# Moving small elementwise work from VectorE to GpSimd, with a new instruction order, in a four-layer attention kernel

## The chip, the cores and the metric

The kernel runs on one core of one Trainium2 chip. The time is that of one execution in device microseconds (us); times below are medians of four executions unless it is said otherwise; the four of the kernel before lie within 0.5% of each other. VectorE (DVE), ScalarE (ACT), GpSimd (POOL) and TensorE (PE, its weight loads PEld) each have a list of instructions of their own, whose order the program fixes. "Granted clock" is the share of full TensorE speed that the records show.

## The reference

The input x has 2048 rows of 512 values and 32 heads of 16. Four layers, A B A B, each add attention(layernorm(x)) to x.

```python
# layer A: linear attention; pk is made from k in the same way
pq = einsum("bhsd,hdf->bhsf", q, w_phi)
phi_q = concat([softmax(pq), softmax(-pq)])
kv = einsum("bhsf,bhsd->bhfd", phi_k, v);  z = sum over s of phi_k      # over all rows
o = einsum("bhqf,bhfd->bhqd", phi_q, kv) / (einsum("bhqf,bhf->bhq", phi_q, z) + 1e-6)
# layer B: a window of 8 earlier rows at distance 0, 2, ... 14
attn = softmax(q . k[rows] * scale);  o = attn . v[rows]
# both
x = x + o @ wo
```

Only kv and z of layer A join all rows. Between these "global sums" a block of 512 rows can run ahead of the others.

## The kernel before

Rows are handled in four blocks b of 512. A step of a stage is a small closure. All steps are emitted in one fixed global order (the string `_ORDER`), which thereby fixes the list of every engine. `_CHOICE` says for each flexible step (emptying a PSUM bank, adding a residual, normalising) whether VectorE or ScalarE does it, and `_SLOTS` gives the buffers.

```python
for w in _ORDER.split():
    key = self.names[int(w, 36)]
    ...
    self.threads[key][i]()

# layernorm of the new x: mean and variance from two accumulated sums
def sq(t):     # ScalarE: sum of squares of a row, by accum_out
    nc.scalar.activation(out=sqd[:], in_=xb[:, t, :], func=ACT.Square, accum_out=T["ss"][:, t:t + 1])
def var(lo, n):
    u = T["sums"][:, lo:lo + n]
    nc.vector.scalar_tensor_tensor(out=q, in0=u, scalar=-1.0 / D, in1=u, op0=ALU.mult, op1=ALU.mult)
    nc.vector.tensor_tensor(out=q, in0=q, in1=ss, op=ALU.add)          # q, ss: slices, shortened here
def ln():      # ScalarE: lnv = Ln(scale * var + eps); rstd = Exp(-lnv / 2)
    ...
def nmr():     # VectorE: the shift, -mean * rstd
    nc.vector.scalar_tensor_tensor(out=U["nmr"][:, 0:n], in0=T["sum"](), scalar=-factor,
                                   in1=U["rstd"][:, 0:n], op0=ALU.mult, op1=ALU.mult)
# keys: sums of 16 exponentials in four levels t8, t4, t2, t1; the last one:
def t1(t, m):
    nc.vector.tensor_tensor(out=T["s1"][:, 0:m * G], in0=T["s2"][:, 0:m * G, 0], in1=T["s2"][:, 0:m * G, 1], op=ALU.add)
# query normaliser: dr multiplies the denominators (PSUM) by rS, then
    nc.vector.tensor_tensor(out=T["Ds"][:], in0=T["DR"][:, 0, :], in1=T["DR"][:, 1, :], op=ALU.add)
def rho():
    nc.vector.tensor_tensor(out=T["rho"][:], in0=self.rS[L, b][:],
                            in1=T["Ds"][:].unsqueeze(1).to_broadcast([P, 2, P]), op=ALU.mult)
```

The large VectorE work of layer B is `prod` (query times shifted keys) and `pav` (weights times shifted values): 128x4096 products, both inputs in SBUF, 2.3 us each and 2.2 us from start to start.

## Time and profile before

| | before |
|---|---|
| median of three executions | 330.5 us (329.39 to 330.88) |
| span of the profiled execution | 327.5 us |
| busy: PE, VectorE, ScalarE, GpSimd | 310.3, 302.2, 279.3, 25.3 us |
| VectorE idle (span less busy) | 25.3 us |

The page and its rows are shown in the prediction.

### The profile page before, as it was taken

The page shows a single profiled execution, that of the slowest core. Times are in us where ns is not written, and L with a number is a line of the kernel's source. Part 1 is how long each engine was busy: PE and PEld are TensorE (multiplying, and loading weights), DVE is VectorE, ACT ScalarE, POOL GpSimd, SP SyncE. Part 2 cuts the span into 40 slices and gives each one's busy share as a digit, 9 for nine tenths or more (in the row PEclk, how much of TensorE's full clock was granted, in tenths as well). Part 3 has the DMA queues.
Part 4 walks back from the last instruction along what each step waited for, and adds up shares of the span by engine and source line. Part 5 has one row for each costly group of instructions (what it writes and reads, how often), then busy time and mean ns, then how long its engine had stood idle before and what let it go on. Part 6 is the DMA issues. An engine that isn't in the chain of part 4 may idle for free. (4 is left out here: it accounts for less than half of the span.)

```text
span 327.5 us, 8033 instructions
## 1 busy us (share of the span) xinstructions
PE 310.3 (95%) x3176; PEld 149.5 (46%) x3203; DVE 302.2 (92%) x439; ACT 279.3 (85%) x634; POOL 25.3 (8%) x50
## 2 busy tenths in 40 slices
PE   7999999999999999999999999979999999999873
PEld 3655456445444444443444455644544454433221
DVE  7998995998998999899999999699999999999993
ACT  5999988998888999989999999798999996676550
POOL 4000000000021003000000000000000208400000
PEclk9999999999999999999999999999999999999999
DMA  7980000004556899998750300023436977679952
GB/s 197 380 197 3 0 2 4 2 20 120 105 148 135 152 164 133 139 121 154 137 135 1 67 3 2 4 59 90 128 58 125 179 146 134 150 139 158 166 176 92
DMA packets 37388, 35.41 MB, mean 108 GB/s; under 512 B 23008, under 2 KB 32224, under 8 KB 37344
## 3 DMA queue, kind: packets, MB, share of 16 engines
q1 hardware_dynamic: 36816, 34.81, 53.6%
q8 instruction: 27, 0.44, 0.6%
q14 instruction: 17, 0.14, 0.2%
q10 hardware_dynamic: 528, 0.02, 0.1%
HBM read 10.50 MB, written 2.36 MB: 39 GB/s over the span
## 5 line engine op out<-in xcount | busy, mean ns | idle before, releaser
L927 PE MATMUL ps<-xnT,WB 128*128 128x512 bf16 x384 | 87.6, 380 | 0.5 <-DMA xnT<-xn 0.5
L1081 DVE TENSOR_TENSOR pav<-PT,Vg 128x4096 bf16<-128x4096 bf16 (+1 forms) x34 | 72.0, 2162 | 1.5 <-DMA Vg<-V 1.0
L1019 DVE TENSOR_TENSOR prod<-QT,K 128x4096 bf16<-128x4096 bf16 x32 | 72.5, 2291 | 0.3 <-ACT QT L192 0.2
L927 PEld LDWEIGHTS <-WB 128*128 128x128 bf16 x384 | 42.3, 114 | 43.3 <-issue 5.8
L520 PEld LDWEIGHTS <-oT 128*128 128x128 bf16 x256 | 23.8, 97 | 34.5 <-ACT oT L192 5.7
L192 ACT CAST oT<-ps 128x512 bf16<-128x512 f32 (+1 forms) x60 | 32.1, 587 | 8.4 <-PE ps L1090 7.1
L706 ACT ACTIVATE Eq<-ps 128x512 bf16<-128x512 f32 x64 | 34.0, 615 | 0.7 <-PE ps L698 0.6
L520 PE MATMUL ps<-WoB,oT 128*128 128x512 bf16 x122 | 32.1, 380 | 2.4 <-ACT oT L192 2.0
L599 ACT ACTIVATE Ek<-ps 128x512 bf16<-128x512 f32 x64 | 33.6, 622 | 0.4 <-PE ps L593 0.2
L698 PE MATMUL ps<-xnT,WA 128*128 128x512 bf16 x128 | 30.7, 380 | 0.6 <-DVE Eq L816 0.6
L540 ACT ACTIVATE sqd<-x 128x512 bf16<-128x512 bf16 x48 | 30.1, 643 | 1.0 <-DVE x L533 0.8
L605 PE MATMUL ps<-WA,xnT 128*128 128x512 bf16 x120 | 30.0, 380 | 0.5 <-issue 0.2
L593 PE MATMUL ps<-WA,xnT 128*128 128x512 bf16 x124 | 29.7, 380 | 0.6 <-DMA xnT<-xn 0.2
L520 PE MATMUL ps<-WoA,oT 128*128 128x512 bf16 x120 | 29.2, 380 | 0.4
L533 DVE SCALAR_TENSOR_TENSOR x<-ps,x 128x512 bf16<-128x512 f32 x38 | 25.4, 686 | 1.9 <-PE ps L520 1.7
L192 ACT CAST V<-ps 128x512 bf16<-128x512 f32 x31 | 17.5, 595 | 4.4 <-PE ps L927 4.3
L192 ACT CAST K<-ps 128x512 bf16<-128x512 f32 x31 | 17.8, 585 | 3.7 <-PE ps L927 3.3
L530 ACT ACTIVATE x<-ps 128x512 bf16<-128x512 f32 x26 | 15.1, 598 | 6.4 <-PE ps L523 6.3
L192 ACT CAST QT<-ps 128x512 bf16<-128x512 f32 x29 | 17.1, 592 | 2.5 <-PE ps L927 2.5
L651 DVE TENSOR_TENSOR Ek<-Ek,rk 128x4096 bf16<-128x4096 bf16 (+1 forms) x10 | 18.6, 1858 | 0.5 <-ACT rk L646 0.5
L593 PEld LDWEIGHTS <-xnT 128*128 128x128 bf16 x128 | 12.1, 97 | 15.4 <-DMA xnT<-xn 0.7
L446 ACT ACTIVATE xn<-x,nmr,rstd 128x512 bf16<-128x512 bf16 x23 | 18.2, 822 | 1.0 <-DVE nmr L435 0.8
(129 smaller groups left out, 433.3 us busy)
## 6 DMA issues: line engine op xcount, KB each, us to landing
Vg<-V SPq DMA_DIRECT2D x128, 131.5 KB, 4.4
Prho<-rd SPq DMA_DIRECT2D x8, 512.0 KB
x<-in_A_x_dram SPq DMA_DIRECT2D x3, 512.0 KB
WB<-in_B_wqkv_dram SPq DMA_DIRECT2D x3, 512.0 KB, 11.6
wraw<-in_A_wqkv_dram SPq DMA_DIRECT2D x4, 256.0 KB, 4.5
out_dram<-x SPq DMA_DIRECT2D x4, 256.0 KB, 2.2
out_dram<-x SPq DMA_DIRECT2D x8, 128.0 KB, 2.2
x<-in_A_x_dram SPq DMA_DIRECT2D x4, 128.0 KB
```

Source lines behind the costliest of these rows:

```text
L192: self.nc.scalar.copy(out=out, in_=in_)
L520: nc.tensor.matmul(y[:], lhsT=oT[:, c, t * P:(t + 1) * P], rhs=Wo()[:, c, :], start=(c == 0), stop=(c == NB - 1 and not onpe))
L533: nc.vector.scalar_tensor_tensor(out=xb[:, t, :], in0=T[t][:], scalar=1.0, in1=xb[:, t, :], op0=ALU.mult, op1=ALU.add, **kw)
L540: nc.scalar.activation(out=sqd[:], in_=xb[:, t, :], func=ACT.Square, accum_out=T["ss"][:, t:t + 1])
L593: nc.tensor.matmul(pk[:], lhsT=xnT[:, t, k, :], rhs=self.WA[:, k, D:2 * D], start=(k == 0), stop=(k == NB - 1))
L599: nc.scalar.activation(out=T["E"][:, t, s, :], in_=T["k", t][:], func=ACT.Exp, scale=1.0 - 2.0 * s)
L605: nc.tensor.matmul(pv[:], lhsT=xnT[:, t, k, :], rhs=self.WA[:, k, 2 * D:3 * D], start=(k == 0), stop=(k == NB - 1))
L698: nc.tensor.matmul(pq[:], lhsT=self.WA[:, k, hb * P:(hb + 1) * P], rhs=xnT[:, :, k, :], start=(k == 0), stop=(k == NB - 1))
L706: nc.scalar.activation(out=self.Eq[L, b][s][:, :, hb, :], in_=T[hb][:].rearrange("p (t i) -> p t i", t=4), func=ACT.Exp, scale=1.0 - 2.0 * s)
L927: nc.tensor.matmul(pp[:], lhsT=self.WB[:, k, i * D + c:(i + 1) * D:NB], rhs=xnT[:, :, k, :], start=(k == 0), stop=(k == NB - 1))
L1019: nc.vector.tensor_tensor(out=pr[:], in0=QT[:, c:c + 1, :].to_broadcast([P, NW, TB]), in1=win, op=ALU.mult)
L1081: nc.vector.tensor_tensor(out=pv, in0=PT[:, :, lo:lo + n].unsqueeze(1).to_broadcast([P, NB, 2, n]), in1=vw, op=ALU.mult)
```

## The change

The intent: VectorE is near full and GpSimd nearly empty, so small elementwise work goes to GpSimd wherever no global sum waits for it. The core of the diff, with cuts:

```diff
         def var(lo, n):
-            nc.vector.scalar_tensor_tensor(out=T["q"]..., in0=u, scalar=-1.0 / D, in1=u, op0=ALU.mult, op1=ALU.mult)
-            nc.vector.tensor_tensor(out=T["q"]..., in0=T["q"]..., in1=T["ss"]..., op=ALU.add)
+                nc.gpsimd.tensor_tensor(out=w, in0=u, in1=u, op=ALU.mult)
+                nc.gpsimd.tensor_scalar(out=q, in0=ss, scalar1=float(D), scalar2=None, op0=ALU.mult)
+                nc.gpsimd.tensor_tensor(out=q, in0=q, in1=w, op=ALU.subtract)     # 12 places; scale 1/(D*D) later
 ...
         def t1(t, m):
+            eng = nc.gpsimd if pl else nc.vector        # pl: b < 3, six places
 ...
+        def ds():
+            eng = nc.gpsimd if pl else nc.vector        # pl: b > 0, six places
         def rho():
+            eng = nc.gpsimd if pl else nc.vector        # six places
 ...
-_ORDER = """ av 8 i i i ...      (the whole string is new)
-_CHOICE = ( "00111111..."        (new: other engines for evictions, residuals and normalisations)
-_SLOTS = { ...                   (new)
```

So there are two changes in one: the moved instructions, and a new order with its own choice of engines. The other edits of the diff remove dead options.

## The prediction

> **What bounds the kernel now.** I read the page's busy table first, then the busy time in stretches, the chain of waits, the groups by line and shape, and last the timelines of VectorE and GpSimd. The busy table and the slices:
>
> ```profile
> span 327.5 us, 8033 instructions
> PE 310.3 (95%) x3176; PEld 149.5 (46%) x3203; DVE 302.2 (92%) x439; ACT 279.3 (85%) x634; POOL 25.3 (8%) x50
> ...
> DVE  7998995998998999899999999699999999999993
> ...
> POOL 4000000000021003000000000000000208400000
> ```
>
> Three engines are near full and GpSimd is nearly empty: that is what the change wants to use. In stretches (columns: length, then busy time and instructions of PE, PEld, DVE, ACT, POOL, then clock and DMA):
>
> ```profile
> 40.00:60.00 20.00, 19.45 (x473) 11.26 (x473) 15.68 (x28) 17.33 (x40) 0.38 (x1) 1.00 0.01 2
> 140.00:160.00 20.00, 19.15 (x138) 8.06 (x134) 19.77 (x21) 18.92 (x47) 0.00 (x0) 1.00 0.85 134
> 260.00:280.00 20.00, 20.00 (x138) 9.46 (x136) 19.91 (x13) 16.46 (x34) 7.18 (x4) 1.00 0.75 137
> 280.00:300.00 20.00, 18.75 (x148) 7.98 (x148) 20.00 (x10) 14.23 (x31) 3.61 (x2) 1.00 0.87 152
> ```
>
> From 260 to 300 us VectorE has not 0.1 us free and sets the pace; at 40 to 60 us, where the key/value sum over all rows (the global sum) is turned into weights, it idles a fifth of the time because it waits. So a microsecond taken from VectorE is worth something in the first kind of stretch and nothing in the second. The chain of waits (from 219 us on) names PE for 26% of the span and VectorE for 3%. I don't take that as a pure PE bound: a 512-column matmul shows 380 ns in the groups, but four of them follow each other every 0.216 us in the chain ("PE ps L520 x4" is 0.86 us), so busy time overstates the array's load. Streaming each matmul's columns at that rate I estimate 284 us of work in 327. PE, VectorE and ScalarE are balanced, and a change must relieve two of them to pay.
>
> **What the Trainium skill says.** "SBUF — State Buffer", section "Who interferes with whom": a VectorE instruction with two SBUF inputs contends with a GpSimd instruction that reads SBUF, and the one that comes second blocks for the whole of the other. This trace agrees. VectorE and GpSimd, from two timelines:
>
> ```profile
> 270.65 2.28 DVE L1081 TENSOR_TENSOR pav<-PT,Vg 128x4096 bf16<-128x4096 bf16 x1
> 272.85 2.32 DVE L1019 TENSOR_TENSOR prod<-QT,K 128x4096 bf16<-128x4096 bf16 x1
> 275.10 2.32 DVE L1081 TENSOR_TENSOR pav<-PT,Vg 128x4096 bf16<-128x4096 bf16 x1
> ```
>
> ```profile
> 249.34 0.23 POOL L969 COPY vh<-V 128x64 bf16<-128x64 bf16 x1
> ...
> 270.79 2.24 POOL L953 COPY K<-K 128x64 bf16<-128x64 bf16 x1 [10.27 <-ACT K L192]
> 272.97 2.30 POOL L969 COPY vh<-V 128x64 bf16<-128x64 bf16 x1
> 275.33 2.18 POOL L965 COPY V<-vh 128x64 bf16<-128x64 bf16 x1
> ```
>
> The same copy takes 0.23 us when VectorE is not in such an instruction and about 2.2 us when it is: it ends as the VectorE product ends, and three copies in a row waited for three products. The cost to VectorE is small: these products start 2.23 to 2.25 us apart, against 2.21 elsewhere, so some 0.03 us a time. Where VectorE has one input in PSUM nothing should block; the page says so, and this trace has no GpSimd work there to test it.
>
> "GPSIMD Engine Reference", section 3.1: an elementwise two-input instruction costs about 2.6 cycles an element (4497 ns for 2048 fp32). No two-input GpSimd instruction is in this trace. As an estimate from that page: 128 elements 0.34 us, 256 elements 0.62 us. For the 4-element ones I take 0.2 us from the unblocked 0.23 us copy.
>
> **The change part by part.** Counts are from comparing the instruction lists of the two kernels per engine; durations from these rows of the groups:
>
> ```profile
> L801 DVE TENSOR_TENSOR rho<-rS,Ds 128x256 bf16<-128x256 f32 x8 | 3.4, 419 | 1.7 <-ACT Ds L797 1.6
> L793 DVE TENSOR_TENSOR Ds<-s 128x128 f32<-128x128 f32 x8 | 2.3, 292 | 0.3
> L552 DVE TENSOR_TENSOR q<-q,ss 128x4 f32<-128x4 f32 x12 | 2.0, 166 | 2.1 <-ACT sqd L540 1.1
> L550 DVE SCALAR_TENSOR_TENSOR q<-sums 128x4 f32<-128x4 f32 x12 | 1.9, 159 | 0.0
> L530 ACT ACTIVATE x<-ps 128x512 bf16<-128x512 f32 x26 | 15.1, 598 | 6.4 <-PE ps L523 6.3
> L533 DVE SCALAR_TENSOR_TENSOR x<-ps,x 128x512 bf16<-128x512 f32 x38 | 25.4, 686 | 1.9 <-PE ps L520 1.7
> L190 DVE COPY xnT<-ps 128x1024 bf16<-128x1024 bf16 (+1 forms) x11 | 7.2, 661 | 0.7 <-PE ps L460 0.6
> ```
>
> Taken from VectorE: variances 12 x (0.159 + 0.166) = 3.9 us; normaliser sums 6 x 0.292 = 1.75; normaliser products 6 x 0.419 = 2.5; last level of key sums 6 x 0.42 (the 256-wide form in the timeline) = 2.5. Together 10.7 us.
>
> But the diff also replaces the instruction order, the buffer slots and the choice of which engine empties PSUM, and the lists show that the free time is spent at once. VectorE gets 9 more evictions of K, Q and V (9 x 0.686 = 6.2), 7.5 more of oT (5.1) and 4 more of xnT (2.4); it gives up 7 residual additions (6 x (0.686 + 0.083), the last a read of the accumulated sum, + 0.7 = 5.3), 3 normalisations (3 x 0.36 = 1.1) and a little at the query products (0.3). That is +7.0, so -3.7 by durations. It also has 31 fewer instructions, and neighbours overlap by about 0.08 us (two residual additions of 0.68 start 0.61 apart), so the durations count 31 x 0.08 = 2.5 us twice: VectorE really gains 1.2 us. By stage, adding the list up at start-to-start times, nothing changes before the second global sum and about 1 us goes from the part after it.
>
> ScalarE gets the 7 residuals (6 x (0.598 + 0.204) + 0.6 = 5.4), 3 normalisations (2.4) and one extra copy (0.6), and gives up 9 evictions (5.3), 7.5 of oT (4.4) and 4 of xnT (3.8): -5.1, or -4.7 with the overlap. PE gets 7 identity matmuls more, since a residual on ScalarE is added in PSUM: 7 x 0.22 = +1.5 us.
>
> GpSimd gets 54 instructions: 36 x 0.2 + 6 x 0.34 + 12 x 0.62 = 16.7 us unblocked, and more with waits of up to 2.2 us each; I expect its busy time at 45 to 75 us. To VectorE this costs 36 x 0.03 = 1.1 us for the small ones. The products and sums of the normaliser run beside products with an input in PSUM and should cost nothing; the 6 key-sum levels sit beside the two-input products of Ek, so I charge half of 6 x 0.62, 1.9 us. Sum on VectorE: -1.2 + 1.1 + 1.9 = about +2; on ScalarE -4.7; on PE +1.5.
>
> Waits: a variance is three GpSimd instructions in series instead of two on VectorE. Before, VectorE waited for the normalisation's exponential 0.3 us in all:
>
> ```profile
> DVE nmr L435 <- ACT rstd L431: 0.3, 1, 0.3
> ```
>
> Now the third instruction can be caught behind one more product, and when VectorE reaches the shift (nmr) it waits for GpSimd, two activations and the signals: 0.2 + 0.2 + 0.3 + 0.2 and some tenths, say 1.2 us. In 6 of the 12 places the new order leaves at most one or two products in between; if half of those wait, 3 to 4 us of VectorE time are lost, part of it refilled by PE and ScalarE running on.
>
> **The rivals.** (a) The plain gain: the order was made anew for the lighter ScalarE and VectorE, so residuals, evictions and transposes come earlier and the gaps in PE's stream (43 us by my estimate) shrink. For it: ScalarE's 4.7 us and a tuned order; about 322 to 325 us. (b) The lock hands the time back: GpSimd waits for products, the shift waits for GpSimd, VectorE idles in the stretches where it is the bound. For it: the 2.2 us copies; about 331 to 336 us. (c) Nothing much: VectorE's and PE's sums move by 1 to 2 us either way and the tail is the same; 327 to 331 us. For it: VectorE's amount by stage is unchanged.
>
> **Range and chances.** The sums alone give about the old time: ScalarE's relief less VectorE's 2 us and PE's 1.5. Against that stands the new order, which fits evictions to where engines are free; I credit it with 3 us, about 1%, the weakest term here. Predicted 327.5 us against 330.5, with 322 to 333 to hold it 8 times in 10. Over 2% faster is under 323.9: 0.17. Over 2% slower is above 337.1 and needs rival (b) at full strength: 0.06. Within 2%: 0.77.
>
> **What would show it.** Busy times of about 299 to 302 for VectorE, 274 for ScalarE and 312 less what the span loses for PE; GpSimd at 45 to 75 us, its 4-element instructions either near 0.2 or near 2.2 us. If the waits of nmr for rstd stay under 2 us in sum, rival (b) is out. If products beside GpSimd work start later than 2.25 us apart, the lock costs more than I charged. If the key-sum instructions take far more than 0.62 us and the keys' reciprocal waits for them, the first 50 us grow. I am wrong if the 260 to 300 us stretch gains idle VectorE time, or if the new order is worth over 7 us by itself.

## More of the kernel before

The sets of experiments ran on different chips, each with its own runs of the kernel before.

For the comparison I also cut the span at the instruction that ends each global sum (the product `R`, which exists twice). The columns are start:end, length, then busy time and instructions of PE, PEld, VectorE, ScalarE and GpSimd, then granted clock, DMA share and GB/s.

```profile
0.00:53.90 53.90, 51.82 (x589) 28.79 (x595) 47.93 (x106) 47.27 (x100) 5.12 (x30) 1.00 0.41 119
53.90:209.50 155.60, 152.68 (x1596) 72.81 (x1608) 145.30 (x204) 144.46 (x337) 7.27 (x11) 1.00 0.53 92
209.50:327.50 118.00, 105.79 (x993) 47.90 (x1001) 108.96 (x132) 87.57 (x200) 12.91 (x9) 1.00 0.62 125
```

In the middle phase VectorE is idle 155.6 - 145.3 = 10.3 us, in the last one 118.0 - 109.0 = 9.0 us.

## The result, and the profile after

| median of four executions | before | changed |
|---|---|---|
| time | 329.96 us (329.39 to 330.88) | 348.48 us (345.68 to 351.9) |

The changed kernel is slower by 18.5 us in medians (17.5 us in the means). The ratio is 1.053, with a 95% interval of 1.046 to 1.060. Here and below a ratio is the mean time of one kernel's runs over that of the other's runs of the same rounds, so not quite the ratio of the medians. Executions over 1.5% slower than the fastest of the same kernel are left out of the means. Of the changed kernel's runs the one at 351.9 us counts as slow and is left out of the ratio; the profiled run is a fast one. The median of its three fast runs is 347.9 us, so differences from 348.5 us below are up to 0.6 us too large.

The page of the changed kernel:

```profile
span 345.9 us, 8066 instructions
PE 317.3 (92%) x3182; PEld 150.8 (44%) x3210; DVE 301.5 (87%) x402; ACT 275.5 (80%) x630; POOL 65.9 (19%) x104
...
DVE  6899996968799798997998699696689989999992
...
POOL 4000000203041642050005201023014240500000
```

VectorE's busy time is the same to 0.7 us (302.2 before), so the 18.4 us of longer span are all idle time of VectorE: 345.9 - 301.5 = 44.4 us, against 25.3 before. Ten of the first 39 slices of its row are at 7 or below and spread over the run; before there were three. The same cut at the two `R`:

```profile
0.00:55.20 55.20, 52.08 (x590) 28.61 (x595) 47.85 (x105) 46.34 (x98) 6.62 (x33) 1.00 0.41 116
55.20:221.00 165.80, 156.50 (x1595) 73.79 (x1608) 145.39 (x183) 142.05 (x332) 38.07 (x44) 0.99 0.51 86
221.00:345.90 124.90, 108.75 (x997) 48.38 (x1007) 108.23 (x118) 87.15 (x202) 21.19 (x27) 0.98 0.64 118
```

The first phase grows by 1.3 us, the middle one by 10.2 and the last by 6.9. In the middle phase GpSimd's 44 instructions take 38 us. What they are (groups; busy time in us and mean ns of one, then GpSimd's own idle time):

```profile
L552 POOL TENSOR_SCALAR q<-ss 128x4 f32<-128x4 f32 x12 | 13.7, 1144 | 11.3 <-ACT sqd L538 11.3
L551 POOL TENSOR_TENSOR qw<-sums 128x4 f32<-128x4 f32 x12 | 12.9, 1073 | 80.7 <-DVE x L531 48.4 <-ACT x L528 32.3
...
L553 POOL TENSOR_TENSOR q<-q,qw 128x4 f32<-128x4 f32 x12 | 4.6, 381 | 1.0
L814 POOL TENSOR_TENSOR rho<-rS,Ds 128x256 bf16<-128x256 f32 x6 | 4.4, 726 | 6.4 <-ACT Ds L809 6.4
L805 POOL TENSOR_TENSOR Ds<-s 128x128 f32<-128x128 f32 x6 | 2.8, 462 | 37.0 <-DVE s L797 22.1 <-DVE rho L814 11.0 <-PE ps L821 3.9
```

The instructions of four elements take 1.1 us on average, though a free one (at 74.25 us) takes 0.20. And this is who waits for them (engine and tile, the one it waited for, total us, times, longest), from the waits of the changed kernel:

```profile
ACT lnv L426 <- POOL q L553: 16.6, 10, 3.0
DVE nmr L433 <- ACT rstd L429: 11.9, 12, 3.4
```

Before, the same two waits were 0.3 us for `nmr` (shown in the prediction) and this for `lnv`:

```profile
ACT lnv L428 <- DVE q L552: 1.9, 7, 0.4
```

One of the chains in order of time, from the timelines of the changed kernel (start, duration, then the instruction, and in brackets the idle time before it and what ended it). GpSimd:

```profile
111.38 2.11 POOL L551 TENSOR_TENSOR qw<-sums 128x4 f32<-128x4 f32 x1 [7.96 <-DVE x L531]
113.67 2.05 POOL L552 TENSOR_SCALAR q<-ss 128x4 f32<-128x4 f32 x1 [0.18 <-ACT sqd L538]
115.80 2.10 POOL L553 TENSOR_TENSOR q<-q,qw 128x4 f32<-128x4 f32 x1
```

VectorE:

```profile
111.15 6.69 DVE L1023 TENSOR_TENSOR prod<-QT,K 128x4096 bf16<-128x4096 bf16 x3
118.50 0.16 DVE L433 SCALAR_TENSOR_TENSOR nmr<-sums,rstd 128x4 f32<-128x4 f32 x1 [0.66 <-ACT rstd L429]
```

ScalarE:

```profile
117.93 0.30 ACT L426 ACTIVATE lnv<-q,eps_t 128x4 f32<-128x4 f32 x1 [2.22 <-POOL q L553]
```

Read them together. Three products stand back to back on VectorE from 111.15 to 117.84. Each of the three GpSimd instructions is caught behind one of them, and a chain with 0.62 us of work when free (0.20 + 0.22 + 0.20 at 74.25 us) takes 6.5 us (111.38 to 117.90). The variance is ready only when the last product ends. ScalarE has stood still for 2.22 us by then, because its queue is in order and `lnv` is at its head; what stands behind it waits too. VectorE then waits another 0.66 us for `nmr`. The Trainium skill, "TensorE: Matmul & The Clock Gate", in the specification table at its top, gives ScalarE's, VectorE's and GpSimd's queues as strictly first in, first out, and the trace agrees: ScalarE's `lnd`, whose matmuls had ended at 115.65 us, ran only behind `lnv` and `rstd`, at 118.37 us. What VectorE makes of it was late in turn:

```profile
119.83 0.69 DVE L1058 TENSOR_TENSOR PT<-E,rden 128x1024 bf16<-128x1024 bf16 x1 [1.17 <-ACT rden L1053]
```

### The profile page after: what moved, and what is told of

Its sections match the earlier page's. It is cut to its first block, busy times and chain, and to the rows that moved or that the text cites. A ratio compares the mean times of both kernels' runs of the same rounds, so it can differ in the third digit from the quotient of the medians.

```text
span 345.9 us, 8066 instructions
## 1 busy us (share of the span) xinstructions
PE 317.3 (92%) x3182; PEld 150.8 (44%) x3210; DVE 301.5 (87%) x402; ACT 275.5 (80%) x630; POOL 65.9 (19%) x104
## 4 chain that ended last, share of the span: by engine, by line
PE 26%; ACT 13%; DVE 10%; POOL 4%; DMA 4%; issue 2%; SPq 0%; DVEq 0%; ACTq 0%; POOLq 0%
PE ps L942 10%; PE ps L518 7%; DMA Vg<-V 4%; PE ps L1094 3%; DVE pav L1085 3%; ACT Ek L604 2%; DVE Eq L829 2%; POOL q L552 2%; POOL qw L551 2%; PE ps L1030 2%; ACT xn L444 1%; PE ps L610 1%; ACT Eq L712 1%; ACT x L528 1%; PE ps L521 1%
## 5 line engine op out<-in xcount | busy, mean ns | idle before, releaser
L1023 DVE TENSOR_TENSOR prod<-QT,K 128x4096 bf16<-128x4096 bf16 x32 | 71.7, 2287 | 2.0 <-ACT K L191 2.0
L191 ACT CAST oT<-ps 128x512 bf16<-128x512 f32 (+1 forms) x52 | 28.7, 586 | 12.1 <-PE ps L1094 8.4
L518 PE MATMUL ps<-WoA,oT 128*128 128x512 bf16 x118 | 31.2, 391 | 1.6 <-ACT oT L191 0.8
L551 POOL TENSOR_TENSOR qw<-sums 128x4 f32<-128x4 f32 x12 | 12.9, 1073 | 80.7 <-DVE x L531 48.4
L1094 PE MATMUL ps<-pav,indAV 128*32 128x512 bf16 (+1 forms) x272 | 19.4, 384 | 8.6 <-DVE pav L1085 6.4
L531 DVE SCALAR_TENSOR_TENSOR x<-ps,x 128x512 bf16<-128x512 f32 x31 | 20.5, 687 | 7.2 <-PE ps L518 6.1
L528 ACT ACTIVATE x<-ps 128x512 bf16<-128x512 f32 x33 | 19.4, 597 | 7.8 <-PE ps L521 7.8
L444 ACT ACTIVATE xn<-x,nmr,rstd 128x512 bf16<-128x512 bf16 x26 | 20.4, 816 | 0.8 <-DVE nmr L433 0.8
L610 PEld LDWEIGHTS <-xnT 128*128 128x128 bf16 x128 | 12.1, 99 | 15.4 <-issue 2.2
L598 PEld LDWEIGHTS <-xnT 128*128 128x128 bf16 x128 | 12.2, 98 | 14.2 <-DVE xnT L189 0.8
## 6 DMA issues: line engine op xcount, KB each, us to landing
WB<-in_B_wqkv_dram SPq DMA_DIRECT2D x3, 512.0 KB, 10.6
```

The source lines that it names most:

```text
L191: self.nc.scalar.copy(out=out, in_=in_)
L518: nc.tensor.matmul(y[:], lhsT=oT[:, c, t * P:(t + 1) * P], rhs=Wo()[:, c, :], start=(c == 0), stop=(c == NB - 1 and not onpe))
L598: nc.tensor.matmul(pk[:], lhsT=xnT[:, t, k, :], rhs=self.WA[:, k, D:2 * D], start=(k == 0), stop=(k == NB - 1))
L610: nc.tensor.matmul(pv[:], lhsT=xnT[:, t, k, :], rhs=self.WA[:, k, 2 * D:3 * D], start=(k == 0), stop=(k == NB - 1))
L1023: nc.vector.tensor_tensor(out=pr[:], in0=QT[:, c:c + 1, :].to_broadcast([P, NW, TB]), in1=win, op=ALU.mult)
L1094: nc.tensor.matmul(po[32 * c:32 * c + 32, lo:lo + n], lhsT=self.indAV[:], rhs=T["p", q][:, c, hf, lo:lo + n], start=(hf == 0), stop=(hf == ...
```

## The experiments

The theories ("port" is short for the contention between VectorE's instructions with two SBUF inputs and GpSimd's reads of SBUF, which the prediction describes):

- **Port.** The variance chain on GpSimd reads SBUF, loses to VectorE's two-input products, and halts ScalarE and VectorE through their queues. Then the time comes back when the chain only writes.
- **Order.** The new order, choice and slots are worse by themselves, wherever the small work runs. Then the time does not come back when GpSimd's work is made harmless, and the old order suffers little from the moved work.
- **Any wait.** A rival to the port: a third engine in the chain, with its signals, costs the time even where nothing blocks.

A kernel named new_order starts from the changed kernel, and one named old_order from the kernel before. Before's median in the same sets, of seven or eight runs, was 329.8 to 329.9 us. The edits are shown in short.

### Which part of the moved work costs, and in which order

**new_order_all_dve** keeps order, choice and slots and runs the same steps on VectorE again.

```diff
-  three nc.gpsimd lines of var;  eng = nc.gpsimd if pl else nc.vector
+  two nc.vector lines of before; eng = nc.vector          # t1, Ds, rho
```

> The new order, slots and eviction choices, with all three kinds of work issued on VectorE again (variance in its old two-instruction form), at the same places of the order. Theory (the serial GpSimd variances behind the lock cost the time): falls from 348 to 329-335 us, the waits of nmr for rstd back under 3 us, ScalarE no longer waiting for q. Rival (the new order and mix of evictions are themselves worse): stays at 340-348 us.

Measured: 357.14 us, ratio 1.082 (1.080 to 1.085), outside both ranges.

**new_order_var_dve** returns only the variances.

```diff
-  three nc.gpsimd lines of var
+  two nc.vector lines of before
```

> The new order, only the variances back on VectorE; key sums and normaliser stay on GpSimd. Theory (variances are the cause): within 2 us of the run with all three back, so 329-336 us. Rival (the larger GpSimd instructions of key sums and normaliser cost VectorE the port): 4 us or more above that run.

Measured: 346.55 us, ratio 1.051 (1.047 to 1.055), 10.6 us below the run with all three back, which neither side had expected. Read alone, these two would say that GpSimd helps and that the order costs 27 us. They are no fair measure of the order. A step that was placed for GpSimd's own queue now sits in VectorE's queue, where everything behind it must wait for its inputs. With the variances back, ScalarE still waits 9.7 us for `q`, and VectorE still waits 5.9 us for `rstd`. I draw nothing from their size except that moving the steps back does not repair the new order.

**old_order_var_pool** puts only the variances on GpSimd, in the order of before.

```diff
-  two nc.vector lines of var, scale 1/D
+  three nc.gpsimd lines of the changed kernel, scale 1/(D*D)
```

> The kernel before with its order unchanged, only the variances as three GpSimd instructions. Theory: the variances alone cost most of the 18 us here too: 340-350 us, ScalarE waiting 10 us or more for q and VectorE 8 us or more for rstd. Rival (only the new order makes the variances late): 330-335 us.

Measured: 334.84 us, ratio 1.016 (1.014 to 1.018): +5.0 us. That is in the rival's range and far below the theory's 340 us, so most of the 18 us needs the new order as well. The middle phase carries the 5 us, 155.60 us before:

```profile
54.30:213.86 159.56, 154.03 (x1596) 73.01 (x1608) 143.68 (x187) 143.41 (x337) 27.83 (x35) 1.00 0.53 89
```

and the waits have the same names as in the changed kernel:

```profile
ACT lnv L428 <- POOL q L555: 12.9, 9, 2.5
DVE nmr L435 <- ACT rstd L431: 9.7, 11, 1.3
```

VectorE is 1.6 us less busy there than before and 5.6 us more idle. So the chain costs time without any new order. The waits, which are those that the theory forecast, sum to more than the 5 us; presumably they overlap and the other engines fill a part, which no run separates.

**old_order_t1_rho_pool** puts only the key sums and the normaliser on GpSimd.

```diff
-  nc.vector.tensor_tensor(... t1 ...);  nc.vector.tensor_tensor(... Ds, rho ...)
+  (nc.gpsimd if b < 3 else nc.vector).tensor_tensor(... t1 ...)
+  (nc.gpsimd if b > 0 else nc.vector).tensor_tensor(... Ds, rho ...)
```

> The kernel before with its order unchanged, key sums' last level (three blocks of four) and the normaliser's sum and product (three of four) on GpSimd, variances left. Theory: 328-333 us, nearly free, for these run where VectorE's neighbours have an input in PSUM. Rival (port contention from the larger instructions): 335 us or more.

Measured: 330.14 us, ratio 1.001 (0.999 to 1.003). `rho` takes 0.727 us and `Ds` 0.461 us on GpSimd, the same as in the changed kernel: nothing blocks them, since they run beside VectorE instructions with an input in PSUM. That is the rule on PSUM inputs which the prediction took from the Trainium skill. The prediction said that its trace could not test it, but it could: the copy of 0.23 us at 249.34 us, which it shows, ran while VectorE added a residual from PSUM (249.07 to 249.76 us). The key-sum level does get blocked here (1.72 us on average, 0.61 free, 2.52 beside the product of the keys, 3.66 at 190.09 us, where a second instruction with two SBUF inputs follows that product), yet the time moves by only 0.3 us. Its reader on ScalarE waits for it 1.2 us in all: a slow instruction costs little where its reader comes late enough.

**old_order_all_pool** is the idea of the change without its order: both of the edits above.

> All three moves to GpSimd in the kernel before's own order, slots and choices: the idea of the change without its new order. If the parts add up (variances +5.0, key sums and normaliser +0.3): 334-336 us, so that the idea itself is a loss of 5 us and the rest of the 18 comes with the new order.

Measured: 337.08 us, ratio 1.023 (1.019 to 1.027). The results are correct, so this is a fair measure of the idea alone: it loses 7 us. The last phase is not touched (117.7 us from the second `R` to the end; 118.0 before); the middle phase is 162.3 us. The two parts measured alone would add to 5.3 us, and the further 2 us are not explained.

### Order and choice crossed

Here the string of choices of one kernel is put into the other, and nothing else.

```diff
 old_order_new_choice:  -_CHOICE of before    +_CHOICE of the changed kernel
 new_order_old_choice:  -_CHOICE of changed   +_CHOICE of before
```

> The kernel before (order, slots and work per engine unchanged) with the new choice of which engine evicts, adds residuals and normalises. Theory (the order itself, fitted to instruction times that the chip doesn't have, is the loss; the mix is harmless): 329-336 us. Rival (the mix is the loss): 340 us or more.

> The changed kernel with the old choice of engines for evictions and residuals. Theory (order): stays at 344-352 us. Rival (mix): falls to 330-338 us.

Measured: 384.32 us (ratio 1.168, 1.162 to 1.173) and 376.34 us (1.145, 1.139 to 1.150; one of its four runs counts as slow). Both lie outside every range and are worse than either kernel by far. Neither order works with the other's choice, so this pair of runs cannot say which of them is at fault. It failed as an experiment.

### Taking the variances away, and taking their reads away

The next kernels give a wrong result. **new_order_const_var** and **old_order_const_var** have no variance work at all; `lnv` reads a constant.

```diff
+  self.vone = const.tile([P, 4], F32);  nc.gpsimd.memset(self.vone[:], float(D))     # once, at the start
-  three (two) instructions of var;  V["var"] = q
+  nothing;                          V["var"] = self.vone
```

> The changed kernel with every variance after the first normalisation replaced by a constant held ready (wrong result on purpose): no variance instruction on any engine, and the logarithm waits for neither GpSimd nor the squares. Theory A (late variances are what the new order can't bear): 330-336 us. Theory B (the new order loses elsewhere as well): 338-344 us. If it stays above 345 the variances don't matter at all.

> The control: the same constant in the kernel before. It frees 3.9 us of VectorE time by durations and every wait on variances, so it is the most that taking variances off VectorE could ever bring in the old order: 326-329.5 us under either theory; under 324 would mean the variances mattered there too.

Measured: 337.71 us (1.022, 1.018 to 1.026), between the two theories' ranges, and 330.06 us (1.002, 1.000 to 1.003). The second is the plainest result: in the kernel before, the variances cost nothing, for removing them wholly gains nothing. In that order the best that the largest part of the move could do was zero. In the new order their removal gives back 10.8 us, down to 7.9 above before.

**new_order_no_reads** and **old_order_no_reads** keep three GpSimd instructions in series with the wait for the sum of squares, but make them write only.

```diff
-  gpsimd: w = u * u;  q = D * ss;  q = q - w
+  gpsimd.memset(w, 1.0);  gpsimd.memset(ss, D);  gpsimd.memset(ss, D)      # lnv reads ss, scale 1/D
```

> The changed kernel with the three GpSimd instructions of each variance replaced by three that only write (memsets, the last two onto the sums of squares, so that they still wait for the squares and the logarithm still waits for them; wrong result on purpose). The chain engine to engine is as long, but nothing of it reads SBUF. Theory (waiting for the port behind VectorE's two-input products is the cost): 337-342 us, near the run with constant variances (337.7), and these instructions take 0.1-0.3 us each. Rival (the mere serial hop squares, GpSimd, logarithm, shift at places where the order leaves nothing in between): 345-349 us.

> The same write-only chain in the kernel before's order, against 334.8 us with the reading one. Theory (port): 329.5-331.5 us. Rival (hops): 333-335 us.

Measured: 336.02 us (1.017, 1.012 to 1.022), 1 us below the theory's range, and 330.46 us (1.001, 0.997 to 1.005). The same place in the new order as above, GpSimd and then VectorE:

```profile
113.75 0.10 POOL L553 MEMSET ss<- 128x4 f32 x1
```

```profile
110.88 6.78 DVE L1023 TENSOR_TENSOR prod<-QT,K 128x4096 bf16<-128x4096 bf16 x3
117.57 0.19 DVE L433 SCALAR_TENSOR_TENSOR nmr<-sums,rstd 128x4 f32<-128x4 f32 x1
```

The memset runs in 0.10 us in the midst of the products, and `nmr` follows the last product with no wait at all. The phases from the first `R` on:

```profile
56.10:211.50 155.40, 153.07 (x1595) 73.53 (x1608) 144.49 (x182) 142.04 (x332) 19.16 (x44) 1.00 0.54 92
211.50:337.30 125.80, 110.80 (x997) 48.60 (x1007) 108.08 (x118) 87.10 (x202) 19.94 (x27) 0.96 0.65 117
```

The middle phase is back at 155.4 us (155.6 before, 165.8 in the changed kernel). This settles two things. The middle phase's 10.2 us are the port's: the same number of GpSimd instructions at the same places, with the same wait for the squares, cost nothing once they don't read SBUF. (A free memset is also 0.1 us shorter than a free reading instruction, which is at most 8 x 0.3 = 2.4 us over the eight chains of this phase.) And the rival "any wait" is out, since signals to and from GpSimd are still there (ScalarE's waits in front of `lnv` for GpSimd shrink from 16.6 to 1.3 us). In medians the reads cost 348.5 - 336.0 = 12.5 us in the new order and 334.8 - 330.5 = 4.4 us in the old one.

The last phase, however, stays at 125.8 us. This alone does not clear the variances' reads of its loss: the profiled run is the slowest of this kernel's four, 339.0 us, some 3 us over its median run, and the granted clock was 0.5 for 10.2 us of this phase, against 3.4 us of it in the changed kernel. Half of such a stretch, 5.1 and 1.7 us, is the most that it can take, as an estimate. The kernel with no variance work at all, new_order_const_var, decides it. Its last phase:

```profile
210.80:336.50 125.70, 108.27 (x997) 48.04 (x1007) 108.07 (x118) 86.91 (x202) 18.77 (x15) 0.97 0.64 117
```

TensorE works there until 329.0 us and has, before that, one stretch of 3.4 us at half clock. So some 6 of the 7.7 us over the 118.0 us of before belong neither to the variances nor to the clock.

**new_order_gpsimd_writes_only** goes to the end of this path: key sums, normaliser and the copies of halo rows become memsets as well.

```diff
 as new_order_no_reads, and
-  gpsimd: t1, Ds, rho;  three tensor_copy of K and V halo rows
+  gpsimd.memset(s1, 64.0), (Ds, 1.0), (rho, 0.0001);  gpsimd.memset(..., 0.0) three times
```

> The changed kernel's order with every GpSimd instruction of the block loop made write-only: the variances as before, and now also the key sums' last level, the normaliser's sum and product and the halo copies are memsets (wrong result on purpose; the normaliser's no longer wait for their inputs, so this is a lower bound). Theory (the some 6 us left after the variances are a second share of the port): 329-331.5 us. Rival (they lie in the order and mix of the last quarter itself): 334-337 us, with the phase after the second global sum still 6 us or more longer than the 118.0 us of before.

Measured: 337.45 us (1.020, 1.015 to 1.026), no better than new_order_no_reads, and with the long last phase that the rival named.

```profile
55.37:210.13 154.76, 152.63 (x1595) 73.44 (x1608) 143.80 (x181) 141.87 (x332) 5.62 (x44) 1.00 0.53 92
210.13:337.80 127.67, 110.22 (x997) 48.54 (x1007) 107.48 (x118) 87.35 (x202) 3.20 (x27) 0.95 0.64 116
```

GpSimd works 3.2 us in the last phase, and that phase is still 127.7 us, where before has 118.0. This profiled run, too, is its kernel's slowest, 339.5 us, 2 us over the median, and half clock for 10.2 us before its very end can take at most 5.1 us; that does not close a gap of 9.7 us. So most of what is lost there is neither the port nor GpSimd's speed. It comes with the new order, choice and slots.

### A try at a better version

**new_order_one_late** is correct and leaves one GpSimd instruction after the sum of squares, by folding the factor D into ScalarE's square.

```diff
-  Square(x), accum ss;                   gpsimd: w = u * u;  q = D * ss;  q = q - w
+  Square(x * sqrt(D)), accum ss;         gpsimd: w = u * u;  q = ss - w
```

> The changed kernel with the factor D folded into ScalarE's square (its scale is the root of D), so that only one GpSimd instruction instead of two stands between the last square and the logarithm (correct result). Theory (port): each of the 12 chains can be caught by one product less, 2.2 us at the some 6 places where that happened: 341-346 us. Rival (hops): 347-349 us.

Measured: 345.80 us (1.047, 1.043 to 1.052). It saves 2.7 us in medians, but its runs (344.34 to 347.06 us) overlap with those of the changed kernel, so even this is not clear of the noise. The groups of the changed kernel say why not more: the third instruction averages 381 ns, and of its 12 places the one shown is the only one where it was caught for a whole product (one more took 0.49 us). The first two are what loses, at over 1 us each. With the folding the subtraction takes the place of the second and is caught in its stead (1.08 us on average). ScalarE still waits 11.6 us for `q` and VectorE 10.0 us for `rstd`.

No version beats the kernel before; the key sums and the normaliser on GpSimd in the old order equal it.

## Why the prediction was wrong, step by step

The time was predicted at 327.5 us with 322 to 333 as the range; it is 348.5 us. The direction was wrong too.

**What held.** Three busy times came out as told: VectorE 301.5 us (299 to 302 predicted), ScalarE 275.5 (274), GpSimd 65.9 (45 to 75); TensorE's did not (317.3 us, against 312 or less). Of the 36 four-element instructions 31 are near 0.2 or near 2.2 us, as told, the others between. The normaliser's work is not blocked beside products from PSUM. The tests named at the end of the prediction did their work: the waits of `nmr` for `rstd` are 11.9 us, not under 2, so rival (b) is in; and rival (b) had the right mechanism. Its chance of 6% was the error, and so was its size.

**First failed step: "3 to 4 us of VectorE time are lost, part of it refilled".** Two of its terms were wrong. It let "the third instruction can be caught behind one more product" stand for the whole chain, and half of six places wait. In fact the first two instructions are the ones that are caught, each by a product of its own: 7 and 6 of the 12, for all or part of a product. And `nmr` waits in 10 of the 12 places, 10.7 us in all (the rest of the 11.9 us is in the first normalisation, which does not use GpSimd). And it counted only VectorE's wait. ScalarE's list stops at `lnv` for 16.6 us, which the prediction did not think of, so the "refill" by PE and ScalarE did not come: in the middle phase TensorE's idle time went from 2.9 to 9.3 us and ScalarE's from 11.1 to 23.8. Write-only instructions at the same places give 12.5 us of the time back, and the whole of the middle phase's 10.2 us.

**Second failed step: "the new order, which fits evictions to where engines are free; I credit it with 3 us".** It costs 5.5 us instead: the new order with the variances' reads gone is at 336.0 us against 330.5 for the same edit in the old order. Most of the loss is in the last phase (118.0 us before; 124.9 changed; 125.8 and 127.7 without reads), where VectorE is as busy as before (108.2 against 109.0) and idle 16.7 us against 9.0. The criterion that I had written down, idle VectorE time from 260 to 300 us, saw little of it: 1.8 us there against 0.1 before. In new_order_const_var, where no variance confuses it, VectorE idles 7.0 us in the first 40 us after the second `R` (2.7 before) and 10.4 us in the last 26 us (5.6 in the last 18 us before); in the 60 us between it is as full as before (0.2 us idle, 0.8 before).

**A premise: "a microsecond taken from VectorE is worth something".** The sum of 3.9 us for the variances was right as busy time and worth nothing as time in the old order: without any variance work it takes 330.06 us.

**Sizes that mattered little.** `Ds` takes 0.46 us instead of 0.34, `rho` 0.73 instead of 0.62; the key sum takes 0.61 when free, as estimated, and 0.80 on average. In the old order these moves together cost 0.3 us. VectorE has 37 instructions fewer, as the prediction's own counts give too, not 31; that makes its overlap term 3.0 us, not 2.5.

**What stays open.** Which of the order, the choice and the slots loses the time of the last phase is not known: crossing order and choice broke both. Nor is the mechanism. The records show stretches of half TensorE clock in the new order that the kernel before has only at its very end: 3.41 us long at 188.6 and 239.8 in the changed kernel, 3.41 us at 231.2 and 6.83 at 316.5 in new_order_no_reads. They go with the loss, but no run separates whether they make a part of it or only follow from TensorE's pauses; by the estimates above they cannot make the whole. The 2 us by which the two moves cost more together than one by one are open as well.

## What to carry to other kernels

Before you move work to GpSimd, ask what VectorE runs beside it: next to products with two SBUF inputs every GpSimd instruction that reads SBUF may wait for a whole product, and a chain of three for three. Count the wait of every engine whose in-order list has a reader of the result, not only that of the engine that you relieve. First delete the work on purpose and time the wrong kernel: if that gains nothing, as here, no better place for it can gain anything in that order; and time the idea in the old order apart from a new order.

## What the Trainium skill lacked or had wrong

- "SBUF — State Buffer", "Who interferes with whom": the rule held in both directions (a reading instruction of four elements 2.05 to 2.11 us beside products, a writing one 0.10 us). It does not say that successive GpSimd readers can each lose to the next product, so that three instructions of 0.2 us took 6.5 us, nor that one reader can lose to two VectorE instructions in a row (3.66 us for a key sum of 0.61); and where it says that ScalarE never waits for anyone there, a reader may miss that ScalarE still waits at the semaphore of an instruction which the port held up (16.6 us at `lnv`).
- "GPSIMD Engine Reference", section 3.1: the slope agrees (0.46 us for 128 and 0.73 us for 256 fp32 elements, 2.1 ns an element; 2.6 cycles at the 1.2 GHz that the section divides by are 2.2 ns). The key sum, 256 elements too but from bf16, takes 0.61 us, so the size alone does not set it. The fixed part does not follow from the section: as an estimate, its 4497 ns for 2048 elements, less 2048 x 2.6 cycles at 1.2 GHz (4437 ns), leave 60 ns, but four elements take 0.20 us, and the line through the two fp32 sizes starts at 0.20 us too. The prediction's estimates for `Ds` and `rho` were short by about that difference (0.12 and 0.11 us).
- "TensorE: Matmul & The Clock Gate", "What's actually happening": the stretches at half clock are 3.41 us or twice that, which is the window that the page states. Its table puts the idle state after at least one idle window of about 3.4 us, and a later section says without a size that short idle times between groups of matmuls bring it too. A size from here: the half clock came at 188.6 us after 3.41 us in which TensorE was busy for 1.20 us, with a longest pause of 1.9 us, and at 239.8 us after 3.41 us with 1.37 us busy.
